# A new order for VectorE's weight work in the first slice, and half of some lower parts on GpSimd

## Chip, cores and metric

One core of one Trainium2 chip. The metric is the device time of one execution in microseconds (us), taken as the median of several runs. The engines are TensorE (PE: matmuls; PEld: its weight loads), VectorE (DVE), ScalarE (ACT), GpSimd (POOL) and SyncE (SP, which here only issues DMAs).

## What is computed

A block-wise linear attention with a decay for each head, whose result goes through a feed-forward layer with a squared ReLU. All is float32.

```python
for b in range(nb):                       # 12 blocks of 64 tokens, B=4, H=8, D=64
    intra = (qb @ kb.T * Dmask) @ vb
    inter = (qb * lam_pow) @ kv_state
    out[block] = intra + inter
    kv_state = lam_block * kv_state + (kb * rev_pow).T @ vb
x = out as (3072 tokens, 512)
h = x @ w_in                              # 512 x 2048
g = max(h, 0) ** 2
return g @ w_out                          # 2048 x 512
```

## The kernel before

TensorE multiplies in a reduced float32 format, so each operand is held as an upper part and a lower part (`wh`, `wl` for the weights, `xh`, `xl` for the activations, `gh`, `gl` for the squared ReLU), and each product is three matmuls. The tokens go through in slices of 512 (4 chunks of 128). The first slice is special: while it runs, the weights are converted too, and stay in SBUF from then on.

The first slice is a loop over 16 units, f = 0 to 15. In unit f TensorE makes the hidden block f (`hidden`, L533: 12 matmuls: four with `wh` and `xh`, four with `wh` and `xl`, and last four with `wl`), then the output products of the unit before (`project`, L563, L564, L568: 12 matmuls, with `gl` in every third), then pieces of the attention of the next slice. ScalarE makes `gh` and the square in three activations (`square`, L540 to L543), VectorE subtracts them to `gl` (`rest`, L548).

Beside this, unit f converts one lot of weights, u = f + 2: block u of w_in and the block of w_out that belongs with it, 128 x 1024 elements. The steps, with their lines in the profile:

- SyncE loads it (`wload`, L116) as 64-bit words, two DMAs of 512 KB; there are two buffers, so the load of lot u + 2 waits until the add of lot u has read its words.
- ScalarE: `first_hi` (L124), `first_lo` (L129).
- VectorE, in place in a tile `A` (every third lot lies in `pw` instead): `clamp` (L137), `shift` (L141), `sign` (L148, reads `raw` and `A`), `rounded` (L154, the add; reads `raw` and `A`).
- ScalarE: `upper` (L160, writes `wh`). VectorE: `lower` (L163, `wl` = `A` - `wh`), one unit behind the first four.

The units come in steps of four (step = f % 4), one chunk t of attention for each four: step 0 fades the state and scales the next keys on GpSimd (`fade_state` L519, `scale_k` L393), step 1 masks scores on VectorE (`masked_by_half`, L218, two instructions) and scales queries on GpSimd (`scale_q`, L401), step 2 finishes the chunk, whose results ScalarE copies out (`attend`, L499, L501, L377: five instructions) behind that unit's upper part, and loads the next chunk's 1 MB, step 3 adds the state on VectorE (`state`, L218) and the lower part of the attention's result (`low`, L378).

Every engine works through its instructions in the order of the program text; nothing reorders them. `turn` (L168) is a GpSimd copy of one element to `mark`: it reads a value that VectorE writes, and so makes what stands behind it on GpSimd wait until VectorE is that far.

Of the kernel before, what the change touches and what calls it, by code (L numbers as in the profile page):

```python
# [7 lines left out]
F32 = mybir.dt.float32  # L8
# [4 lines left out]
ALU = mybir.AluOpType  # L13
# [6 lines left out]
NCB = S // C  # L20
NT = B * NCB
DM = H * D
DF = 2048
KT = DM // P
NF = DF // P
# [6 lines left out]
NLOT = NF + 1  # L32
# [3 lines left out]
def body(ctx: ExitStack, tc: tile.TileContext, qT, kT, kvq, lam, w, out):  # L36
    nc = tc.nc
# [9 lines left out]
    V = nc.vector  # L47
# [47 lines left out]
    wh = const.tile([P, 2 * NF, DM], F32R, name="wh")  # L95
    wl = const.tile([P, 2 * NF, DM], F32R, name="wl")
# [4 lines left out]
    def lot(t, u):  # L101
        if u in (0, NF):
            return t[:, u : u + 1]
        return t.rearrange("p (s f) d -> p s f d", s=2)[:, :, u]
# [30 lines left out]
    def clamp(u):  # L135
        A = cv[u][2].bitcast(F32)
        V.tensor_scalar(out=A, in0=A, scalar1=2.0**-15, scalar2=float(LIM), op0=ALU.max, op1=ALU.min)  # L137

    def shift(u):
        A = cv[u][2]  # L140
        V.tensor_scalar(  # L141
            out=A, in0=A, scalar1=3, scalar2=0x3FFFFFFF,
            op0=ALU.logical_shift_left, op1=ALU.bitwise_and,
        )

    def sign(u):
        L, Hw, A = cv[u]
        V.scalar_tensor_tensor(  # L148
            out=A, in0=Hw, scalar=0xC0000000, in1=A, op0=ALU.bitwise_and, op1=ALU.bitwise_or
        )  # L150

    def rounded(u):
        L, Hw, A = cv[u]
        V.tensor_tensor(out=A, in0=A, in1=L, op=ALU.add)  # L154

    def whole(u):
        return cv[u][2].bitcast(F32).rearrange("p (a d) -> p a d", d=DM)

    def upper(u):
        nc.scalar.copy(lot(wh, u), whole(u))  # L160

    def lower(u):
        V.tensor_tensor(out=lot(wl, u), in0=whole(u), in1=lot(wh, u).bitcast(F32), op=ALU.subtract)  # L163
        cv.pop(u)

    def turn(u, half):
        x = cv[u][2].bitcast(F32)[0:1, 0:1] if half else wl[0:1, u, 0:1].bitcast(F32)
        nc.gpsimd.tensor_copy(mark[:, 0:1], x)  # L168
# [11 lines left out]
    def where(x, base, pattern, step, compare, fill):  # L180
# [17 lines left out]
        out=pz[:, C - T : C - T + NX], data0=s[:, 0:1].broadcast_to([P, NX]), data1=spike,  # L198
# [13 lines left out]
    for j in range(2):  # L212
# [5 lines left out]
        lambda o, x, y, op=op: V.tensor_tensor(out=o, in0=x, in1=y, op=op)  # L218
# [5 lines left out]
    b_, t_, u_, c_, d_, af = (sq[:, i, 0 : NS - 1] for i in range(6))  # L224
# [11 lines left out]
    for k in range(NS - 3, NS):  # L236
        n = 1 << k
        V.tensor_scalar(
            out=pz[:, Z + n : Z + 2 * n], in0=pz[:, Z : Z + n], scalar1=tr[:, k : k + 1], scalar2=None,
# [150 lines left out]
    def scale_k(t):  # L390
        x = tok[t][0].rearrange("p (a j) d -> p a j d", j=2)
        y = mask[:, 2:4].rearrange("p j a c -> p a j c")[:, :, :, D - 1 : D]
        nc.gpsimd.tensor_tensor(out=x, in0=x, in1=y.broadcast_to([P, NPR, 2, D]), op=ALU.mult)  # L393

    def scale_q(t):
        x = feat[t][:, 1].rearrange("p a (b c) -> p a b c", b=2)
        if t % NCB:
            y = qpow[:, 0].unsqueeze(2).broadcast_to([P, NPR, 2, D])
        else:
            x, y = x[:, :, 1], qpow[:, 0]  # L400
        nc.gpsimd.tensor_tensor(out=x, in0=x, in1=y, op=ALU.mult)  # L401
# [52 lines left out]
    def begin(t):  # L454
        begun_of[t] = [ps_a.tile([P, DM], F32, name="att") for _ in range(2)], set()
        old_state(t, 0)

    def begun_mark(t):
        c = (NPR - 1) * D
        nc.scalar.copy(mark[:, 2:3], begun_of[t][0][0][0:1, c : c + 1])  # L460
# [43 lines left out]
    def state(t, second, fades=True):  # L504

        if not second and t % NCB == NCB - 1:
            return
        u = part_of.pop(t)[:, NPR * D :].rearrange("p (a b) -> p a b", a=NPR)
        d = kv[:, :, D:] if second else kv[:, :, 0:D]
        if second and not t % NCB:  # L510
            V.tensor_copy(d, u)
        else:
            add(d, kvd, u)
        if fades and (not second or t % NCB < NCB - 1):
            fade_state(second)

    def fade_state(second):
        d = kv[:, :, D:] if second else kv[:, :, 0:D]
        nc.gpsimd.tensor_tensor(  # L519
            out=kvd, in0=d, in1=qpow[:, 0, :, D - 1 : D].broadcast_to([P, NPR, D]), op=ALU.mult  # L520
        )
# [3 lines left out]
    def hidden(m, f, xh, xl):  # L525
        h = ps_h.tile([P, N], F32, name="h")
        k = 0
        order = ((wh, xh), (wl, xh), (wh, xl))
        if m == 0 and f:
            order = order[0], order[2], order[1]  # L530
        for wt, x in order:
            for kt in range(KT):
                nc.tensor.matmul(  # L533
                    h, wt[:, f, kt * P : (kt + 1) * P], x[:, kt], start=k == 0, stop=k == 11
                )
                k += 1
        return h

    def square(h):
        nc.scalar.activation(h, h, AF.Relu)  # L540
        gh = wk.tile([P, N], F32R, name="gh")
        nc.scalar.activation(gh, h, AF.Square)
        nc.scalar.activation(h, h, AF.Square)  # L543
        return gh

    def rest(m, f, r, gh):
        gl = wk.tile([P, N], F32R, name="gl")
        V.tensor_tensor(out=gl, in0=r, in1=gh.bitcast(F32), op=ALU.subtract)  # L548
        g_of[m, f] = gh, gl
# [39 lines left out]
    def new_low(m):  # L589
        xs_of[m].append(wk.tile([P, KT, N], F32R, name="xl", tag="xl"))  # L590
# [436 lines left out]
    o, u, low = {}, {}, {}  # L1027
# [65 lines left out]
    for f in range(NF):  # L1093
        t, step, u_ = G + f // 4, f % 4, f + 2
        h = hidden(0, f, *xs_of[0])
        if step == 2:
            begin(t)
        if f == 2:
            gh = square(h)
            begun_mark(t)  # L1100
            upper(u_ - 1)
        if f < 3:
            if f < 2:
                lower(u_ - 1)
            clamp(u_)
            shift(u_)
            if f == 2:
                lower(u_ - 1)
            if f == 1:
                turn(u_, True)  # L1110
                masked_by_half(t)
                scale_q(t)
                scale_k(t + 1)
                state(t, True)
            sign(u_)
            if f != 1:
                rounded(u_)
        else:
            if u_ < NLOT:
                for op in (clamp, shift, sign):  # L1120
                    op(u_)
            if step < 3:
                upper(u_ - 1)
            if u_ < NLOT:
                rounded(u_)
            if f == 3:
                new_low(1)
            if step == 1:
                gh = square(h)
                turn(u_, True)  # L1130
                scale_q(t)
                rest(0, f, h, gh)
                masked_by_half(t)
            lower(u_ - 1)
            if u_ - 1 < NF and step != 1:
                turn(u_ - 1, False)
            if step == 3:
                state(t, False)
        wload(u_ + 2)
        if f == 0:  # L1140
            fade_state(False)
        if step == 0 and f:
            if t % NCB < NCB - 1:
                fade_state(True)
            scale_k(t + 1)
        if f < 2 or f > 2 and step != 1:
            gh = square(h)
            if step == 2:
                begun_mark(t)
        if f == NF - 1:  # L1150
            state(t + 1, True)
        if step != 1 or f == 1:
            rest(0, f, h, gh)
        if step == 3:
            low[t]()
            if f < NF - 1:
                state(t + 1, True, False)
        if f == 1:
            rounded(u_)
        if f == 0:  # L1160
            upper(u_)
        if u_ + 1 < NLOT:
            first_hi(u_ + 1)
            first_lo(u_ + 1)
        if step == 2 and u_ < NLOT:
            upper(u_)
        if prev is not None:
            project(*prev)
        prev = (0, f)
        if step == 2:  # L1170
            low[t] = attend(t)
            load_qk(t + 2)
            load_kv(t + 2)
        if f == 0:
            open_half(t)
        elif step == 0:
            scores_by_half(t, ps_a, "att")
        if f == NF - 1:
            scores_by_half(t + 1, ps_a, "att")
            scale_k(t + 2)  # L1180
# [14 lines left out]
    for j, tag in enumerate(("xh", "xl")):  # L1195
        x = wk.tile([P, 4, DM], F32, name="raws", tag=tag)
# [6 lines left out]
    def pair(i):  # L1203
        return i, first_t + 2 * i
# [6 lines left out]
    for f in range(NF):  # L1211
        t = first_t + f // 2
        h = hidden(1, f, *xs_of[1])
        behind(f, t, last_t)
        gh = square(h)
# [13 lines left out]
        if f == NF - 1:  # L1229
            x = far(*pair(3))  # L1230
# [4 lines left out]
        if f % 2 == 0:  # L1235
            go(t, t + 1 if t < last_t else None, False)
            if t == last_t:
                x = near(*pair(3), "a")
# [28 lines left out]
    for f in range(NF):  # L1267
        t = first_t + f // 2
        i, odd_ = f // 4, f // 2 % 2
        more = t < last_t  # L1270
# [95 lines left out]
```

## Time and profile before

| | |
|---|---|
| median of 3 runs | 588.33 us (586.6 to 589.16) |
| the profiled execution | 586.28 us, span 584.5 us |
| busy in the span | TensorE 572.0, VectorE 418.7, ScalarE 278.8, GpSimd 94.2 us |
| first slice, 40 to 120 us | TensorE 75.6, VectorE 77.5, ScalarE 63.6, GpSimd 12.0 of 80 us |
| 120 to 160 us | TensorE 40.0 of 40, VectorE 18.4 |
| TensorE's granted clock | 0.999 of full |
| weights' loads (`raw`) | 30 of 512 KB, 4.5 us from issue to landing (median) |
| attention loads | 512 KB (`kv_sb`) and twice 256 KB (`qk_sb`) a chunk |

A timeline row gives start, duration, engine, line and operation, written tile and read tiles, shape, and in brackets the idle time of the engine ahead of it with what ended it. Durations of neighbours overlap a little, since an instruction's record ends when its result is out; the distance from start to start is what the engine needs. Rows of several matmuls give their number behind an x.

### The profile page before, as it was taken

What the parts mean: (1) busy time and instruction counts of PE and PEld (TensorE: products, weight loads), DVE (VectorE), ACT (ScalarE), POOL (GpSimd) and SP (SyncE); (2) the same over time, 40 slices, a digit from 0 to 9 for tenths busy, and PEclk for the clock granted to TensorE, in tenths of its full rate; (3) what the DMA queues carried; (4) which work ended last, traced back from release to release, by engine and by line L of the source; (5) the groups of instructions that cost most, each with busy time, mean ns of one, the idle gap of its engine ahead of it and who ended that gap; (6) DMA issues with size and microseconds to landing.
All of it is one profiled execution on the core that took longest, in us unless ns stands there. A gap on an engine that the chain in (4) does not pass through costs nothing.

```text
span 584.5 us, 13119 instructions
## 1 busy us (share of the span) xinstructions
PE 572.0 (98%) x5276; PEld 481.7 (82%) x5276; DVE 418.7 (72%) x685; ACT 278.8 (48%) x529; POOL 94.2 (16%) x110
## 2 busy tenths in 40 slices
PE   9999899999999999999999999999999999999996
PEld 7976687778888887888888887888788888999996
DVE  5899999952688675786666668677645456997933
ACT  4698778744454455433333334445523244641510
POOL 4530110222322231000000013355100000000000
PEclk9999999999999999999999999999999999999999
DMA  8874566324599795566666643732297676766863
GB/s 298 339 254 164 183 243 217 108 74 145 197 304 351 241 305 194 159 191 208 198 199 197 199 162 121 266 123 74 74 315 230 194 195 184 248 214 204 286 206 105
DMA packets 69388, 119.35 MB, mean 204 GB/s; under 512 B 6352, under 2 KB 30928, under 8 KB 69328
## 3 DMA queue, kind: packets, MB, share of 16 engines
q1 hardware_dynamic: 66864, 115.37, 60.1%
q10 hardware_dynamic: 2464, 3.15, 1.5%
q8 instruction: 42, 0.69, 0.5%
q14 instruction: 18, 0.15, 0.1%
HBM read 88.08 MB, written 29.36 MB: 201 GB/s over the span
## 4 chain that ended last, share of the span: by engine, by line
PE 70%; DVE 19%; issue 4%; ACT 3%; DMA 2%; SPq 0%; DVEq 0%; POOL 0%; ACTq 0%; POOLq 0%
PE h L697 18%; PE acc L945 8%; PE att L697 7%; PE acc L563 6%; PE h L533 6%; PE acc L564 6%; PE acc L568 6%; PE att L945 4%; DVE wl L163 3%; PE att L440 2%; DVE A L148 2%; PE h L945 2%; DVE sums L218 2%; DVE gl L548 1%; DMA raw<-in_w 1%
## 5 line engine op out<-in xcount | busy, mean ns | idle before, releaser
L563 PE MATMUL acc<-wh,gh 128*128 128x512 f32 x256 | 101.1, 395 | 0.0
L568 PE MATMUL acc<-wh,gl 128*128 128x512 f32 x256 | 99.9, 390 | 0.0
L564 PE MATMUL acc<-wl,gh 128*128 128x512 f32 x256 | 99.8, 390 | 0.0
L697 PE MATMUL h<-wh,ring 128*128 128x512 f32 x320 | 85.8, 390 | 0.1
L540 ACT ACTIVATE h<-h 128x512 f32<-128x512 f32 x48 | 27.9, 582 | 107.3 <-PE h L533 49.0
L697 PEld LDWEIGHTS h<-wh,ring 128*128 128x128 f32 x320 | 59.9, 188 | 13.2 <-issue 0.5
L548 DVE TENSOR_TENSOR gl<-h,gh 128x512 fp32r<-128x512 f32 x48 | 33.0, 687 | 37.1 <-ACT h L543 37.1
L568 PEld LDWEIGHTS acc<-wh,gl 128*128 128x128 f32 x256 | 48.0, 188 | 11.0 <-DVE gl L548 0.9
L563 PEld LDWEIGHTS acc<-wh,gh 128*128 128x128 f32 x256 | 48.1, 188 | 10.4
L564 PEld LDWEIGHTS acc<-wl,gh 128*128 128x128 f32 x256 | 48.1, 188 | 9.6
L697 PE MATMUL h<-wl,ring 128*128 128x512 f32 x160 | 49.2, 389 | 0.0
L393 POOL TENSOR_TENSOR kv_sb<-kv_sb,pw 128x512 f32<-128x512 f32 x17 | 22.2, 1306 | 126.6 <-DMA kv_sb<-in_kvq 126.5
L519 POOL TENSOR_TENSOR kvd<-kv,pw 128x256 f32<-128x256 f32 x33 | 27.1, 822 | 83.6 <-DVE kv L218 75.2
L533 PE MATMUL h<-xh,wl 128*128 128x512 f32 x128 | 35.0, 395 | 4.4 <-DVE wl L163 4.4
L533 PE MATMUL h<-xh,wh 128*128 128x512 f32 x128 | 36.5, 407 | 0.5 <-DVE pw L218 0.2
L945 PE MATMUL acc<-folds,wh 128*128 128x256 f32 x192 | 35.2, 283 | 0.0
L697 PEld LDWEIGHTS h<-wl,ring 128*128 128x128 f32 x160 | 30.0, 188 | 6.3
L533 PE MATMUL h<-xl,wh 128*128 128x512 f32 x128 | 34.3, 390 | 0.0
L697 PE MATMUL att<-wh,ring 128*128 128x512 f32 x128 | 34.2, 389 | 0.0
L533 PEld LDWEIGHTS h<-xh,wl 128*128 128x128 f32 x128 | 23.6, 188 | 11.4 <-DVE wl L163 6.5
L218 DVE TENSOR_TENSOR wl<-sums,wh 128x1024 fp32r<-128x1024 f32 x24 | 30.4, 1265 | 1.8 <-ACT wh L917 1.8
L945 PEld LDWEIGHTS acc<-folds,wh 128*128 128x128 f32 x192 | 30.0, 192 | 0.0
(276 smaller groups left out, 1188.5 us busy)
## 6 DMA issues: line engine op xcount, KB each, us to landing
ring<-ws SPq DMA_DIRECT2D x112, 256.0 KB, 3.0
folds<-wt SPq DMA_DIRECT2D x64, 256.0 KB, 3.6
raw<-in_w SPq DMA_DIRECT2D x30, 512.0 KB, 4.5
kv_sb<-in_kvq SPq DMA_DIRECT2D x19, 512.0 KB, 5.7
ws<-parts SPq DMA_DIRECT2D x32, 256.0 KB, 4.5
qk_sb<-in_kT SPq DMA_DIRECT2D x20, 256.0 KB, 4.3
qk_sb<-in_qT SPq DMA_DIRECT2D x20, 256.0 KB, 4.4
out_x<-o SPq DMA_DIRECT2D x16, 256.0 KB, 5.1
```

What stands on the lines that cost most here:

```text
L163: V.tensor_tensor(out=lot(wl, u), in0=whole(u), in1=lot(wh, u).bitcast(F32), op=ALU.subtract)
L218: lambda o, x, y, op=op: V.tensor_tensor(out=o, in0=x, in1=y, op=op)
L393: nc.gpsimd.tensor_tensor(out=x, in0=x, in1=y.broadcast_to([P, NPR, 2, D]), op=ALU.mult)
L519: nc.gpsimd.tensor_tensor(out=kvd, in0=d, in1=qpow[:, 0, :, D - 1 : D].broadcast_to([P, NPR, D]), op=ALU.mult)
L533: nc.tensor.matmul(h, wt[:, f, kt * P : (kt + 1) * P], x[:, kt], start=k == 0, stop=k == 11)
L540: nc.scalar.activation(h, h, AF.Relu)
L548: V.tensor_tensor(out=gl, in0=r, in1=gh.bitcast(F32), op=ALU.subtract)
L563: nc.tensor.matmul(accs[m][i], gh[:, cs], wh[:, j], start=f == 0, stop=False)
L564: nc.tensor.matmul(accs[m][i], gh[:, cs], wl[:, j], start=False, stop=False)
L568: nc.tensor.matmul(accs[m][i], gl[:, cs], wh[:, j], start=False, stop=end)
L697: nc.tensor.matmul(bank, x[:, part_, kt], t[:, q + kt], start=start and z == 0, stop=stop and z == 5, skip_group_check=True,)
L945: nc.tensor.matmul(bank[:, r * 2 * P : (r + 1) * 2 * P], x, y, start=n == 0 and r == 0 and z == 0, stop=n == NQ - 1 and z == 2, skip_group ...
```

## The change

For units f >= 3 the work is written in a new order. VectorE: clamp and shift of the new lot, lower part of the last lot, sign of the new lot, `gl`, and the add at the end. The GpSimd work of each unit comes behind a `turn` that reads the new lot's tile after the shift. In steps 2 and 3 of units in which a new lot is made (f = 3, 6, 7, 10, 11, 14), GpSimd forms the w_out half of the lower part in two instructions of 128 x 256, and VectorE only the w_in half. Units 0 to 2 and everything behind the first slice stay. The line numbers move: lower is L169 on VectorE and L167 on GpSimd, `gl` L554, `turn` L174.

```diff
--- before.py
+++ after.py
@@ -159,8 +159,14 @@
     def upper(u):
         nc.scalar.copy(lot(wh, u), whole(u))
 
-    def lower(u):
-        V.tensor_tensor(out=lot(wl, u), in0=whole(u), in1=lot(wh, u).bitcast(F32), op=ALU.subtract)
+    def lower(u, shared=False):
+        x, y, z = lot(wl, u), whole(u), lot(wh, u).bitcast(F32)
+        if shared:
+            for c in range(0, DM, DM // 2):
+                cs = slice(c, c + DM // 2)
+                nc.gpsimd.tensor_tensor(out=x[:, 1, cs], in0=y[:, 1, cs], in1=z[:, 1, cs], op=ALU.subtract)
+            x, y, z = x[:, 0], y[:, 0], z[:, 0]
+        V.tensor_tensor(out=x, in0=y, in1=z, op=ALU.subtract)
         cv.pop(u)
 
     def turn(u, half):
@@ -1116,45 +1122,47 @@
             if f != 1:
                 rounded(u_)
         else:
-            if u_ < NLOT:
-                for op in (clamp, shift, sign):
-                    op(u_)
             if step < 3:
                 upper(u_ - 1)
-            if u_ < NLOT:
-                rounded(u_)
+            more = u_ < NLOT
+            if more:
+                clamp(u_)
+                shift(u_)
+                turn(u_, True)
+            if step == 0:
+                if t % NCB < NCB - 1:
+                    fade_state(True)
+                scale_k(t + 1)
+            elif step == 1:
+                scale_q(t)
+            lower(u_ - 1, step > 1 and more)
+            if more:
+                sign(u_)
+            if step == 3:
+                state(t, False)
             if f == 3:
                 new_low(1)
+            gh = square(h)
+            if step == 2:
+                begun_mark(t)
+            if f == NF - 1:
+                state(t + 1, True)
+            rest(0, f, h, gh)
             if step == 1:
-                gh = square(h)
-                turn(u_, True)
-                scale_q(t)
-                rest(0, f, h, gh)
                 masked_by_half(t)
-            lower(u_ - 1)
-            if u_ - 1 < NF and step != 1:
-                turn(u_ - 1, False)
+            if more:
+                rounded(u_)
             if step == 3:
-                state(t, False)
+                low[t]()
+                if f < NF - 1:
+                    state(t + 1, True, False)
         wload(u_ + 2)
         if f == 0:
             fade_state(False)
-        if step == 0 and f:
-            if t % NCB < NCB - 1:
-                fade_state(True)
-            scale_k(t + 1)
-        if f < 2 or f > 2 and step != 1:
+        if f < 3 and f != 2:
             gh = square(h)
-            if step == 2:
-                begun_mark(t)
-        if f == NF - 1:
-            state(t + 1, True)
-        if step != 1 or f == 1:
+        if f < 3:
             rest(0, f, h, gh)
-        if step == 3:
-            low[t]()
-            if f < NF - 1:
-                state(t + 1, True, False)
         if f == 1:
             rounded(u_)
         if f == 0:
```

VectorE before, the add of unit 6's lot and then unit 7 (lot in `A`; `wl<-pw` is the lower part of the lot before):

```order
L154 ISA pw<-raw,pw 128x2048
L163 TENSOR_TENSOR wl<-A,wh 128x2x512
L548 TENSOR_TENSOR gl<-h,gh 128x512
L137 TENSOR_SCALAR A<-A 128x1024
L141 TENSOR_SCALAR A<-A 128x1024
L148 SCALAR_TENSOR_TENSOR A<-raw,A 128x1024
L154 ISA A<-raw,A 128x2048
L163 TENSOR_TENSOR wl<-pw,wh 128x2x512
L548 TENSOR_TENSOR gl<-h,gh 128x512
```

VectorE now, unit 6's end and unit 7:

```order
L148 SCALAR_TENSOR_TENSOR pw<-raw,pw 128x1024
L554 TENSOR_TENSOR gl<-h,gh 128x512
L154 ISA pw<-raw,pw 128x2048
L137 TENSOR_SCALAR A<-A 128x1024
L141 TENSOR_SCALAR A<-A 128x1024
L169 TENSOR_TENSOR wl<-pw,wh 128x512
L148 SCALAR_TENSOR_TENSOR A<-raw,A 128x1024
L554 TENSOR_TENSOR gl<-h,gh 128x512
L154 ISA A<-raw,A 128x2048
```

The lower part has moved from behind the add to between shift and sign and has half its size here; the add (ISA) has moved to the end, behind `gl`.

GpSimd before, units 5 to 9 (the three marks are those of units 6, 7 and 8, each behind a lower part):

```order
L401 TENSOR_TENSOR qk_sb<-qk_sb,pw 128x512
L168 COPY mark<-wl 1x1 x3
L519 TENSOR_TENSOR kvd<-kv,pw 128x256
L393 TENSOR_TENSOR kv_sb<-kv_sb,pw 128x512
L168 COPY mark<-pw 1x1
L401 TENSOR_TENSOR qk_sb<-qk_sb,pw 128x4x64
```

GpSimd now, units 5 to 9:

```order
L407 TENSOR_TENSOR qk_sb<-qk_sb,pw 128x512
L174 COPY mark<-pw 1x1
L167 TENSOR_TENSOR wl<-A,wh 128x256 x2
L174 COPY mark<-A 1x1
L167 TENSOR_TENSOR wl<-pw,wh 128x256 x2
L174 COPY mark<-A 1x1
L525 TENSOR_TENSOR kvd<-kv,pw 128x256
L399 TENSOR_TENSOR kv_sb<-kv_sb,pw 128x512
L174 COPY mark<-pw 1x1
L407 TENSOR_TENSOR qk_sb<-qk_sb,pw 128x4x64
```

Two pieces of `wl` stand behind the marks of units 6 and 7, and every mark now reads the lot's tile, not `wl`.

ScalarE's order is the same in both. From unit 6 to unit 7, with the first conversion pair of lot 9, the upper part of lot 8 (which waits for that lot's add) and the attention's copies ahead of unit 7's activations:

```order
L124 ACTIVATE A<-raw 128x1024
L129 ACTIVATE raw<-raw 128x1024
L160 CAST wh<-pw 128x2x512
L505 COPY a<-att 128x2x64
L507 COPY a<-att 64x2x64 x2
L505 COPY a<-att 128x2x64
L507 COPY a<-att 64x2x64 x2
L383 CAST xh<-a 128x4x128
L546 ACTIVATE h<-h 128x512
```

Nothing has moved here but the moment at which VectorE has the upper part's input ready.

## Rows read from the trace of the kernel before

**Rows 1.** Windows: length, busy us of PE, PEld, DVE, ACT, POOL, clock, DMA share, GB/s.

```profile
40.00:120.00 80.00, 75.60 (x639) 58.90 (x638) 77.47 (x92) 63.55 (x99) 12.01 (x22) 1.00 0.51 178
```

**Rows 2.** TensorE's waits, 40 to 75 us, then 75 to 120: sum, times, longest.

```profile
PE h L533 <- DVE wl L163: 3.2, 3, 2.1
...
PE h L533 <- DVE wl L163: 1.2, 2, 0.9
```

**Rows 3.** Timeline of TensorE: `wl` matmuls of units 6, 7; `gl` reads; unit 14.

```profile
65.94 1.20 PE L533 MATMUL h<-xh,wl 128*128 128x512 f32 x4 [2.10 <-DVE wl L163]
...
73.68 1.07 PE L533 MATMUL h<-xh,wl 128*128 128x512 f32 x4
...
80.48 0.39 PE L568 MATMUL acc<-wh,gl 128*128 128x512 f32 x1
...
105.78 0.39 PE L568 MATMUL acc<-wh,gl 128*128 128x512 f32 x1
...
114.34 1.07 PE L533 MATMUL h<-xh,wh 128*128 128x512 f32 x4
```

**Rows 4.** Timeline of VectorE: unit 2 in part, unit 4, masks of unit 5.

```profile
41.12 0.69 DVE L141 TENSOR_SCALAR A<-A 128x1024 uint32<-128x1024 uint32 x1
41.73 1.22 DVE L163 TENSOR_TENSOR wl<-A,wh 128x1024 fp32r<-128x1024 f32 x1
42.86 1.22 DVE L148 SCALAR_TENSOR_TENSOR A<-raw,A 128x1024 uint32<-128x1024 uint32 x1
...
52.86 0.68 DVE L137 TENSOR_SCALAR A<-A 128x1024 f32<-128x1024 f32 x1
53.58 0.69 DVE L141 TENSOR_SCALAR A<-A 128x1024 uint32<-128x1024 uint32 x1
54.31 1.23 DVE L148 SCALAR_TENSOR_TENSOR A<-raw,A 128x1024 uint32<-128x1024 uint32 x1
55.67 1.23 DVE L154 CUSTOM_DVE_ANT_0 A<-raw,A 128x2048 uint16<-128x2048 uint16 x1
56.81 1.22 DVE L163 TENSOR_TENSOR wl<-pw,wh 128x1024 fp32r<-128x1024 f32 x1
57.95 0.69 DVE L548 TENSOR_TENSOR gl<-h,gh 128x512 fp32r<-128x512 f32 x1
58.55 1.35 DVE L137 TENSOR_SCALAR A<-A 128x1024 f32<-128x1024 f32 x1
...
63.77 0.75 DVE L218 TENSOR_TENSOR a<-att,pw 128x256 f32<-128x256 f32 x2
```

**Rows 5.** Timeline, VectorE and GpSimd side by side in unit 1; GpSimd alone, unit 5.

```profile
36.38 1.66 DVE L148 SCALAR_TENSOR_TENSOR A<-raw,A 128x1024 uint32<-128x1024 uint32 x1
...
35.68 1.28 POOL L401 TENSOR_TENSOR qk_sb<-qk_sb,pw 128x512 f32<-128x512 f32 x1
36.93 2.04 POOL L393 TENSOR_TENSOR kv_sb<-kv_sb,pw 128x512 f32<-128x512 f32 x1
...
58.16 0.17 POOL L168 COPY mark<-wl 1x1 f32<-1x1 f32 x1 [6.10 <-DVE wl L163]
58.30 1.05 POOL L393 TENSOR_TENSOR kv_sb<-kv_sb,pw 128x512 f32<-128x512 f32 x1
```

**Rows 6.** Timeline of ScalarE: upper part to last activation of unit 3; conversions.

```profile
45.37 1.05 ACT L160 CAST wh<-A 128x1024 fp32r<-128x1024 f32 x1 [1.63 <-DVE A L154]
...
49.63 0.60 ACT L543 ACTIVATE h<-h 128x512 f32<-128x512 f32 x1
...
61.86 1.18 ACT L124 ACTIVATE pw<-raw 128x1024 f32<-128x1024 f32 x1 [0.84 <-DMA raw<-in_w]
...
63.95 1.04 ACT L160 CAST wh<-A 128x1024 fp32r<-128x1024 f32 x1
```

**Rows 7.** Instructions of tile `raw`, 30 to 125 us: the loads' time to landing.

```profile
DMA to landing us min/median/max: 3.3/4.5/6.1
```

## The prediction

> **What bounds the kernel now.** I read the stages first. Between 40 and 120 us VectorE is busy for 77.5 of 80 us and TensorE for 75.6 [rows 1]; this is the first slice from its 2nd hidden unit to its 14th, in which every unit makes one lot of weights. Behind 122 us TensorE hardly waits for anybody, so whatever it gains before that it keeps to the end. Then the waits of TensorE: all of them in that stretch are for `wl`, the lower parts that VectorE writes, 3.2 us in three before 75 us and 1.2 us in two behind it [rows 2]. The longest is in unit 6, and after each the four matmuls need 1.20 us where undisturbed ones need 1.07 [rows 3]. The most that any order of VectorE can give back here is therefore 4.4 + 5 x 0.13 = 5.0 us.
>
> Why `wl` is late: VectorE does clamp, shift, sign, add on the new lot and only then the lower part of the last one [rows 4]. In units 5, 9 and 13 even `gl` and the two masks stand in front of it.
>
> **What the new order does, term by term.** I call R(f) the moment at which the add of unit f ends. One row pair gives what two dependent instructions cost: clamp to shift 0.72, shift to sign 0.73, sign to add 1.36, while shift to an independent lower part takes 0.61 and lower part to sign 1.13 [rows 4]. An add to the next, independent, instruction takes 1.14, and I take 1.14 for sign to `gl`, which is independent too. So a plain unit goes from 5.69 us (52.86 to 58.55 [rows 4]) to 0.72 + 0.61 + 1.13 + 1.14 + 0.60 + 1.15 = 5.35 us: 0.34 us saved, because no step follows its own input directly. The lower part ends 2.5 us into the unit, not 5.1, and `gl` starts at 3.6. That alone removes the three waits before 75 us: 3.2 + 3 x 0.13 = 3.6 us gained for TensorE.
>
> **GpSimd's halves.** Half a lower part is half of 1.13, so 0.55 us off VectorE in six units. But VectorE and GpSimd hold each other up. GpSimd's `qk_sb` runs from 35.68 for 1.28 us, VectorE's sign, started at 36.38, takes 1.66 instead of 1.23, and GpSimd's next multiply takes 2.04 where it needs 1.05 alone: each stands until the other's whole instruction is over, and the one that waits gets the next turn [rows 4, 5]. So a half on GpSimd costs VectorE what it saves, unless it falls beside `gl` (0.60 us), whose input in PSUM was not held up by anything. Who goes first behind the lower part decides. If the one-element mark copy (0.17 us [rows 5]) also has to wait for the lower part's end, sign comes directly behind it and the real GpSimd work falls beside `gl`: 0.17 us lost a unit, 0.6 where the 1.05 multiply overhangs `gl` by 0.45. If it doesn't, GpSimd's first operation stands in line during the lower part and goes ahead of sign: 0.5 to 1.28 us a unit. No row shows a mark copy beside an instruction of this kind. I take the first, since all the other GpSimd operations do wait, and keep the second as a bound. The Trainium skill, SBUF — State Buffer, section "SBUF: two separate sides", says that the port pair is an exclusive lock, held for a whole instruction, also between a VectorE operation with two SBUF inputs and a GpSimd operation that reads SBUF. The trace agrees (1.66 for 1.23), and by that rule the mark copy, which reads one element, waits too; where it holds, the sum is the first one, otherwise the second.
>
> **What is late next.** The add moves to the unit's end, and two things hang on it. The load of the lot after next takes the buffer that the add releases: it is asked for at R. From the add's end at 55.67 + 1.23 = 56.90 to the ScalarE instruction that waited for that load it is 4.96 us (61.86), and the two conversions take 2.09 (to 63.95) [rows 4, 6]. Then ScalarE's upper part (1.05, the first row of [rows 6]) must come before the lower part. So lower(f+2) starts no earlier than R(f) + 4.96 + 2.09 + 1.05 = R(f) + 8.1. Before, the add ended 4.0 us into the unit, not 5.4 (52.86 to 56.90 [rows 4]), and this chain had slack. In units 7 and 11 ScalarE has more in line: behind the upper part stand the five attention copies and the three activations, 4.86 us from 45.37 to 50.23 with nothing between [rows 6]. There `gl` starts at R(f) + 4.96 + 2.09 + 4.86 = R(f) + 11.9, and the add ends 0.60 + 1.23 later.
>
> Now the sum, with the first bound and in brackets the second. I leave unit 4 starting where it does, 52.9. It lasts 5.35 + 0.6 (1.05); unit 5 reaches its add's end after 0.72 + 0.61 + 1.13 + 1.14 + 0.60 + 0.66 for the masks [rows 4] + 1.23 = 6.1, plus 0.17 (1.28): R(5) = 65.1 (66.7). `gl` of unit 7 starts at 77.0 (78.6) and ends 0.69 later, 77.7 (79.3). TensorE reads it at 80.48 now [rows 3] and would like it 3.6 us sooner, 76.9: it waits, and 2.8 (1.2) us of its gain are left. Four units on: R(7) = 78.8 (80.4). R(9) = R(7) + 8.1 + 1.13 + 1.14 + 0.60 + 0.66 + 1.23 + 0.17 (0.7) = 91.8 (94.0). `gl` of unit 11 ends 12.6 later, 104.4 (106.6), against 105.78 now: 1.4 (-0.8) left. So these four units take 26.7 us in the new order; TensorE without waits needs 105.78 - 80.48 less the one wait between, about 24.9. R(11) = 105.5 (107.7). The upper part of lot 14 is there 8.1 later, 113.6 (115.8); TensorE begins that unit at 114.34 now: 0.7 (-1.5) left. Last comes the wait in unit 14, 0.9 of the 1.2 us [rows 2], with its restart 1.05: the lower part is then ready before it is read, so this is gained in full. Total 1.8 (-0.5). Where GpSimd's multiply blocks the clamp of unit 9, some 0.6 us more is lost. I take **1.5 us gained**.
>
> The profiled execution is 586.28 us (span 584.5), 2.05 below the median 588.33. The sum makes 584.8 of it, and 586.8 of the median.
>
> **Rivals.** (a) *TensorE loses none of it.* If the loads land faster than the one I could time, ScalarE has upper part 8 ready earlier and the chain never binds. The quickest landing is 3.3 us against a median of 4.5 [rows 7]; 1.2 us less in each of the four steps from R(5) to lot 14 is 4.8, more than is lacking. Then all 5.0 us come: 583.3. For it: all waits now are for `wl`, and that moves by 2.5 us. Against it: 4.96 us was measured on a load with no other traffic near.
>
> (b) *GpSimd goes ahead of sign in every unit*: the brackets, 0.5 us slower, 588.8.
>
> (c) *Slower: the loads land late.* The longest landing is 6.1 us [rows 7]. The weights are now asked for nearer to the 1 MB of attention loads that SyncE issues in the same unit. With 1.6 us more in each of four steps the gain of 1.5 becomes a loss of 4.9: 593.2. It decides from some 1.1 us a step on, a landing of 5.6. Against it: only one load in four is near the attention's.
>
> **How the numbers follow.** Forecast 0.45, (a) 0.22, (b) 0.24, (c) 0.09. This kernel's measurement tells some 0.5% (2.9 us) from no change. Faster by more needs 585.4: (a) and the near edge of the forecast, 0.30. Slower by more needs 591.3: (c), 0.09. The rest, 0.61. For 8 in 10 the range takes in (a) and (b) with the runs' own spread of 1.3 us either way, and leaves (c) out: 583.2 to 590.0.
>
> **What the changed profile would show.** Step by step: TensorE's waits for `wl` between 40 and 75 us gone; a plain unit on VectorE near 5.4 us; instead VectorE's `gl` in units 7 and 11 waits for ScalarE's activation by about 1.5 us or more; the ScalarE conversions wait for the weights' DMA, which they hardly did; TensorE waits for `gl` and for the upper part there, about 3 us in sum; SyncE's issue of the weights stands at the end of a unit. Wrong would be: VectorE without idle time in units 7 and 11 (then (a)), sign of 1.8 us and more behind every lower part (then (b)), conversions that start over 6 us after the add (then (c)), or TensorE waiting after 125 us where it does not now.

## The result: slower

The changed kernel takes 592.84 us (median of 5 runs, 591.88 to 593.6) against 587.26 for the kernel before: 1.0084 times as long, 95% interval 1.0061 to 1.0106. I had forecast 586.8, which was 1.5 us under the 588.33 known then, and a range up to 590.0. The profiled execution takes 592.87 us with a span of 591.1, 6.6 longer than the 584.5 of before.

Most of it is in the first slice: unit 15's first matmul starts at 128.87 us, before at 123.06, which is 5.8 of the 6.6 us. Behind it the execution is 0.8 us longer than before (462.2 against 461.4); I have not followed that. The waits of TensorE from 20 to 170 us (instruction and tile, who was waited for: sum, times, longest), to be held against [rows 2]:

```profile
PE att L446 <- DVE a L224: 4.5, 3, 1.7
PE att L446 <- ACT mark L466: 2.7, 3, 1.8
PE acc L574 <- DVE gl L554: 2.5, 3, 1.3
PE h L539 <- DVE pw L224: 0.2, 1, 0.2
```

The waits for `wl`, 4.4 us before, are all gone, as the new order meant. In their place stand 9.7 us for other things in that slice. The largest is one that my prediction doesn't name: `a L224`, the masks of units 5, 9 and 13. `ACT mark` is a copy of one element out of the bank in which an attention has begun, which ScalarE makes behind the activations of units 6, 10 and 14; the attention's next matmuls write that bank and wait for it. The waits for `gl` are for that of units 4, 8 and 12.

VectorE and GpSimd in unit 4, as [rows 4] and [rows 5] show them for before (start, duration, instruction; rows of the two engines apart):

```profile
53.28 0.69 DVE L137 TENSOR_SCALAR A<-A 128x1024 f32<-128x1024 f32 x1
54.00 0.69 DVE L141 TENSOR_SCALAR A<-A 128x1024 uint32<-128x1024 uint32 x1
54.61 1.22 DVE L169 TENSOR_TENSOR wl<-pw,wh 128x1024 fp32r<-128x1024 f32 x1
55.90 2.07 DVE L148 SCALAR_TENSOR_TENSOR A<-raw,A 128x1024 uint32<-128x1024 uint32 x1
57.89 0.68 DVE L554 TENSOR_TENSOR gl<-h,gh 128x512 fp32r<-128x512 f32 x1
58.49 1.21 DVE L154 CUSTOM_DVE_ANT_0 A<-raw,A 128x2048 uint16<-128x2048 uint16 x1
59.63 0.68 DVE L137 TENSOR_SCALAR A<-A 128x1024 f32<-128x1024 f32 x1
...
54.83 1.04 POOL L174 COPY mark<-A 1x1 f32<-1x1 f32 x1 [3.60 <-DVE A L141]
55.83 1.05 POOL L399 TENSOR_TENSOR kv_sb<-kv_sb,pw 128x512 f32<-128x512 f32 x1
```

The mark copy, 0.17 us elsewhere, takes 1.04: it stands until the lower part (54.61 to 55.83) is over. Then GpSimd's multiply starts at once, and sign, 1.23 us by itself, takes 2.07: it stands until that multiply is over at 56.88. Sign overwrites the tile that the mark reads, so it also waits for the mark: it starts 1.29 us behind the lower part's start (in [rows 4] 1.13), and 0.07 behind the multiply's. So the unit lasts 6.35 us, not 5.35 and not 5.69. In unit 6, with GpSimd's two halves:

```profile
68.17 0.69 DVE L169 TENSOR_TENSOR wl<-A,wh 128x512 fp32r<-128x512 f32 x1
68.93 2.42 DVE L148 SCALAR_TENSOR_TENSOR pw<-raw,pw 128x1024 uint32<-128x1024 uint32 x1
...
68.39 0.50 POOL L174 COPY mark<-pw 1x1 f32<-1x1 f32 x1 [4.95 <-DVE pw L141]
68.86 1.41 POOL L167 TENSOR_TENSOR wl<-A,wh 128x256 fp32r<-128x256 f32 x2
```

Both halves run in front of sign: VectorE saves 0.53 us on the lower part and loses 1.2 on sign. Over the units 3 to 13 sign takes 1.74 to 2.65 us, where before it took 1.22 or 1.23; the excess is 10.3 us in sum.

What the moved add does is seen in the chain of work that ended last, within 58 to 79 us (start, length, what):

```profile
58.57 1.14 DVE A L154
...
59.78 0.33 SPq L116
...
60.16 4.64 DMA raw<-in_w
...
64.88 1.14 ACT pw L124
66.01 1.07 ACT raw L129
67.08 0.24 SPq L116
...
67.37 4.81 DMA raw<-in_w
...
72.25 1.14 ACT A L124
73.39 1.06 ACT raw L129
74.44 0.93 ACT wh L160
```

It is the chain of the prediction: add, issue of the load, landing, two conversions, upper part, and then the attention's copies and activations up to the `gl` of unit 7 at 79.18. At 67.08 the view follows the second of the load's two DMAs and puts it to the conversion that ended just then; the first is issued at 67.00, behind the add of unit 5, which ended at 66.93. ScalarE waits for the weights' DMA 13.5 us in seven places; before, it was 1.3 in three, of which [rows 6] shows the longest.

### The profile page after: what moved, and what is told of

It is laid out like the page before. It is cut to its first block, busy times and chain, and to the rows that moved or that the text cites. A ratio compares the mean times of both kernels' runs of the same rounds, so it can differ in the third digit from the quotient of the medians.

```text
span 591.1 us, 13124 instructions
## 1 busy us (share of the span) xinstructions
PE 572.5 (97%) x5276; PEld 482.4 (82%) x5276; DVE 423.2 (72%) x685; ACT 278.5 (47%) x529; POOL 112.2 (19%) x122
## 4 chain that ended last, share of the span: by engine, by line
PE 71%; DVE 12%; ACT 6%; DMA 5%; issue 4%; POOL 1%; SPq 0%; DVEq 0%; ACTq 0%; POOLq 0%
PE h L703 18%; PE acc L951 7%; PE att L703 7%; PE h L539 6%; PE acc L569 6%; PE acc L574 6%; PE acc L570 6%; PE att L951 4%; DMA raw<-in_w 3%; PE att L446 2%; DMA ws<-parts 2%; PE h L951 2%; DVE sums L224 1%; DVE A L154 1%; DVE gl L554 1%
## 5 line engine op out<-in xcount | busy, mean ns | idle before, releaser
L554 DVE TENSOR_TENSOR gl<-h,gh 128x512 fp32r<-128x512 f32 x48 | 32.9, 686 | 39.0 <-ACT h L549 39.0
L569 PEld LDWEIGHTS acc<-wh,gh 128*128 128x128 f32 x256 | 48.1, 188 | 10.3
L399 POOL TENSOR_TENSOR kv_sb<-kv_sb,pw 128x512 f32<-128x512 f32 x17 | 20.8, 1221 | 127.8 <-DMA kv_sb<-in_kvq 127.7
L224 DVE TENSOR_TENSOR wl<-sums,wh 128x1024 fp32r<-128x1024 f32 x24 | 30.4, 1265 | 1.8 <-ACT wh L923 1.8
L548 ACT ACTIVATE gh<-h 128x512 fp32r<-128x512 f32 x48 | 28.8, 599 | 1.5
```

The source lines that it names most:

```text
L569: nc.tensor.matmul(accs[m][i], gh[:, cs], wh[:, j], start=f == 0, stop=False)
```

## Experiments

Three theories. **P**, the port: GpSimd's work behind shift holds up sign. **L**, the loads: the add at the unit's end makes loads and conversions late. **M**, the masks: TensorE waits for them since the next attention begins in the banks of PSUM (the memory that TensorE writes) that they read. The kernel before ran beside each, at 586.6 to 587.1 us median; ratios are against it.

| run | what is changed | median us | ratio, 95% |
|---|---|---|---|
| the change | | 592.84 | 1.0061 to 1.0106 |
| e1_no_half | change without GpSimd's halves | 591.31 | 1.0055 to 1.0105 |
| e17_mark_apart | change, sign doesn't wait for the mark | 591.52 | 1.0055 to 1.0108 |
| e4_masks_early | change, masks behind shift | 591.04 | 1.0048 to 1.0092 |
| e11_no_loads | change, loads of lots 9 to 16 left out | 590.30 | 1.0047 to 1.0083 |
| e3_pool_late | change, GpSimd's work behind sign | 588.14 | 1.0007 to 1.0031 |
| e5_pool_late_no_half | e3 without halves | 587.32 | 0.9991 to 1.0030 |
| e16_late_no_loads | e3, loads of lots 9 to 16 left out | 584.76 | 0.9959 to 0.9984 |
| e9_beside_gl | no halves; masks and scale_q behind shift, other GpSimd work behind sign | 589.11 | 1.0026 to 1.0055 |
| e10_add_first | e9, add ahead of gl | 587.52 | 1.0006 to 1.0032 |
| e19_q_by_masks | e3, masks and scale_q behind the lower part | 589.45 | 1.0027 to 1.0069 |
| e18_mixed | e19 without halves, add ahead of gl in half of the units | 588.24 | 1.0013 to 1.0042 |
| e2_half_only | before, with GpSimd's halves | 588.86 | 1.0019 to 1.0049 |
| e15_before_step1 | before; in units 5, 9, 13 masks and scale_q behind shift, lower part ahead of gl | 587.16 | 0.9993 to 1.0019 |

### One part alone, and one part away

**e1_no_half**: the call without its second argument.

```diff
-            lower(u_ - 1, step > 1 and more)
+            lower(u_ - 1)
```

> The changed kernel with VectorE writing the whole lower part in every unit, GpSimd's halves left out; the order and the marks as changed. Theory P (the port: what GpSimd has in line behind the mark goes ahead of sign and holds it up): sign in units 3, 6 and 14 falls from 2.4 to about 1.7 us, in 7, 10, 11 from 1.75 to 1.6, the lower part rises from 0.69 to 1.22; in sum VectorE neither gains nor loses, 591.5 to 593.5, and steps 0 and 1 keep their sign of 2.1 to 2.6. Theory L (the add at the unit's end makes the loads late and that is all of the loss): no change either, 592 to 593. If the halves themselves are the loss: back to 587.

4.3 us slower than before, against 5.6: within its error the halves neither make nor mend the loss. Sign in unit 6 fell to 1.22 (no GpSimd work is left behind that mark), the lower part rose to 1.22; in steps 0 and 1 sign stayed at 1.74 to 2.65. The direction is theory P's, though sign fell further than the 1.7 that I expected, and the time is just under my range. The time alone does not divide P from L, which expected no change either.

**e2_half_only**: the old order, with `lower(u_ - 1, step > 1 and u_ < NLOT)`.

> The kernel before with GpSimd's halves alone, VectorE in its old order (and GpSimd's marks as before). The halves are ready to run from the upper part on, beside clamp, shift, sign and add. Theory P: each of the two holds up VectorE by some 0.55 us, 1.1 lost for 0.55 saved in six units: 1 to 4 us slower than before, 588 to 591. Theory L: the add stays where it was, so no slower than before, 584 to 588.

1.9 us slower. TensorE's waits for `wl` rise from 4.4 to 5.4. In the old order the halves run beside shift and sign of the next lot; the pair starts at 93.34:

```profile
93.81 1.11 DVE L141 TENSOR_SCALAR A<-A 128x1024 uint32<-128x1024 uint32 x1
94.95 1.64 DVE L148 SCALAR_TENSOR_TENSOR A<-raw,A 128x1024 uint32<-128x1024 uint32 x1
...
93.34 2.16 POOL L167 TENSOR_TENSOR wl<-pw,wh 128x256 fp32r<-128x256 f32 x2 [1.57 <-ACT wh L160]
```

Shift loses 0.42 and sign 0.41, against 0.54 saved on the lower part, as theory P expected.

### GpSimd's work behind sign

**e3_pool_late**: mark, fades, scalings and halves (`lower_rest`) move down by two VectorE instructions.

```diff
                 clamp(u_)
                 shift(u_)
+            lower(u_ - 1, step > 1 and more)
+            if more:
+                sign(u_)
                 turn(u_, True)
             if step == 0:
...
             elif step == 1:
                 scale_q(t)
-            lower(u_ - 1, step > 1 and more)
-            if more:
-                sign(u_)
+            if step > 1 and more:
+                lower_rest(u_ - 1)
```

> The changed kernel with the mark, all GpSimd work of the unit and the halves behind sign instead of behind shift, so that they start beside gl; VectorE's order as changed. Theory P: sign falls to 1.23 us everywhere, the add or the next clamp is held up instead by what is left over; a unit is 0.5 to 1 us shorter, gl and masks come sooner: 586 to 589. Theory L: the add still ends the unit and the loads are as late: 590 to 593.

1.2 us slower than before, so 4.4 of the 5.6 us are back by this move alone. Unit 4 again:

```profile
56.27 1.22 DVE L148 SCALAR_TENSOR_TENSOR A<-raw,A 128x1024 uint32<-128x1024 uint32 x1
57.41 0.68 DVE L559 TENSOR_TENSOR gl<-h,gh 128x512 fp32r<-128x512 f32 x1
58.01 1.89 DVE L154 CUSTOM_DVE_ANT_0 A<-raw,A 128x2048 uint16<-128x2048 uint16 x1
...
57.76 1.05 POOL L404 TENSOR_TENSOR kv_sb<-kv_sb,pw 128x512 f32<-128x512 f32 x1
```

Sign is 1.22 in all units. The multiply hides beside `gl` as far as `gl` lasts, and the add takes the rest (1.89 instead of 1.22). The masks are early enough now. What TensorE still waits for:

```profile
PE att L451 <- POOL qk_sb L412: 3.0, 3, 1.2
PE att L451 <- ACT mark L471: 2.9, 4, 1.3
PE h L544 <- ACT wh L160: 0.7, 2, 0.4
PE acc L579 <- DVE gl L559: 0.4, 1, 0.4
```

`qk_sb` are the queries, whose scaling the move has made late; the next two come through ScalarE. P holds for most of the loss, though not all of the 4.4 us is its own: with shorter units the adds, and so the loads, come sooner too (unit 5's add ends at 66.11, in the changed kernel at 66.93).

**e5_pool_late_no_half**: the same without halves.

> The kernel of e3_pool_late (mark and GpSimd's work behind sign) with VectorE writing the whole lower part in every unit, no halves. It asks what the halves are worth where GpSimd's work doesn't stand in front of sign. If they save VectorE 0.55 us in six units and fall beside gl: e5 is 1 to 2.5 us slower than e3_pool_late, 589 to 590.5. If what they save comes back as an add held up (1.5 us and more instead of 1.22): the same as e3_pool_late, 587.5 to 588.7.

587.32 against 588.14, with intervals that overlap: where GpSimd doesn't stand in front of sign, no gain from the halves shows. A part of the 0.53 us that one saves comes back in the add (1.50 to 1.56 us in units 3, 6 and 10 with them, 1.22 without).

**e17_mark_apart**: the mark of the changed kernel reads a copy, so that sign, which overwrites what the mark reads, has no wait for it.

```diff
+    def note(u):
+        V.tensor_copy(mark[:, 3:4], cv[u][2].bitcast(F32)[0:1, 0:1])
+        nc.gpsimd.tensor_copy(mark[:, 0:1], mark[:, 3:4])
...
-                turn(u_, True)
+                note(u_)
```

> The changed kernel, but the mark no longer reads the lot's tile, which sign writes: VectorE copies one element of it to a place of its own behind shift, and the mark reads that. GpSimd's work stands where it did, only sign waits for nobody any more. Theory W (sign waits for the mark, since it overwrites what the mark reads; the mark waits for the lower part's end, and the work behind the mark starts before the signal is back at VectorE): sign now gets in behind the mark, 1.3 to 1.4 us in most units instead of 1.75 to 2.65; of the 4.5 us that moving GpSimd's work behind sign gave back at least half comes back here, at a price of about 0.2 us a unit for the copy: 588 to 590.5. Theory P alone (whoever waited longer gets the port, marks or not): sign stays at 1.75 to 2.65 and the copies come on top: 593 to 595.

4.7 us slower, between the two forecasts: theory W, the wait, is not the whole cause. Without it sign gets in first in units 3, 4 and 12 (1.21 us) and in no other (1.76 to 2.80). VectorE's signs of units 4 and 5, and GpSimd's marks there:

```profile
56.07 1.21 DVE L148 SCALAR_TENSOR_TENSOR A<-raw,A 128x1024 uint32<-128x1024 uint32 x1
...
62.06 2.44 DVE L148 SCALAR_TENSOR_TENSOR A<-raw,A 128x1024 uint32<-128x1024 uint32 x1
...
55.14 2.18 POOL L178 COPY mark<-mark 1x1 f32<-1x1 f32 x1 [3.78 <-DVE mark L177]
...
61.06 1.11 POOL L178 COPY mark<-mark 1x1 f32<-1x1 f32 x1 [2.73 <-DVE mark L177]
```

At 56.07 sign starts on time and the mark stands until it is over as well (2.18); at 62.06 it is the other way round. Both wait for the same lower part. In the three units in which sign came first the mark starts 0.20 us after the lower part has begun, in the six in which all GpSimd work did, 0.13 or 0.14. Why this should decide stays open. In the changed kernel that distance is 0.22, so there the wait for the mark may have its share; no run shows how much.

### The loads

**e11_no_loads**: the lots from 9 on take the words of lots 7 and 8 instead of a load; **e16_late_no_loads** does the same to e3.

```diff
+            if u > 8:
+                raw[u] = kept_raw[7 + (u - 9) % 2][:, 0 : len(x) * DM]
+                return
...
+            kept_raw[u] = raw[u]
```

> The changed kernel with the loads of the lots 9 to 16 left out: the words of lots 7 and 8 are converted again, so w_in and w_out are wrong from there on; nothing else changes. ScalarE's conversions then wait for no DMA. Theory L: what came from late loads goes, that is TensorE's waits for ScalarE's mark (2.7 us) and what VectorE idled (about 6 us from unit 7 to 13): 587 to 589.5. Theory P: VectorE is as long behind shift as before and stays the bound: 591 to 593.

> The kernel of e3_pool_late (GpSimd's work behind sign) with the loads of lots 9 to 16 left out, so that lots 7 and 8 are converted again and the weights are wrong from there on. Theory P and L together (the two are the whole loss): what e3_pool_late still waits for ScalarE's mark (2.9 us) and the upper part (0.7) shrinks to 1 us or less, scale_q's 3.0 us stay: 584.5 to 586.5. Theory P alone (the loads cost nothing by themselves): as e3_pool_late, 587.5 to 588.5.

Without loads the change is still 3.7 us slower than before (a gain of 1.9 on the change): too slow for L alone, faster than P alone allows. e16 is 584.76, 3.4 us faster than e3 and 2.1 faster than before. So leaving the loads out is worth some 2 us while GpSimd keeps sign back (the intervals of this run and the change overlap) and 3.4 once it doesn't. TensorE's waits in e16:

```profile
PE att L455 <- ACT mark L475: 2.1, 3, 1.4
PE att L455 <- POOL qk_sb L416: 1.4, 2, 1.0
PE h L548 <- ACT wh L164: 0.3, 1, 0.3
```

Its unit 15 starts at 122.07 on TensorE, 1.0 us before the old kernel's 123.06. The span is 1.8 shorter; where the other 0.8 comes from behind unit 15 I have not followed. These two runs also take the loads' traffic away, not only their lateness, and the kernel before was not run without loads, so they bound what L costs and do not measure it.

### Masks, queries and the add's place

**e4_masks_early** moves `masked_by_half(t)` from behind `gl` to between shift and lower part.

> The changed kernel with the two masks of units 5, 9 and 13 between shift and lower part instead of behind gl. TensorE waited 4.5 us for these masks in the changed kernel. Theory M (the masks free the PSUM banks in which the next unit's attention begins, so where they stand decides): these waits are gone, and since scale_q runs beside the masks sign falls to 1.3 us there: 587 to 589.5. Theory L: the waits move to the next thing that VectorE is late with: 591 to 593.

4.1 us slower, 1.5 better than the change. The masks' waits are gone, as theory M says:

```profile
PE att L446 <- ACT mark L466: 5.0, 3, 2.7
PE acc L574 <- DVE gl L554: 1.9, 2, 1.1
PE h L539 <- DVE wl L169: 1.4, 2, 0.7
```

But the total, 8.3, is nearly the old 9.7: the next late things take their place. Sign is 1.21 in units 5, 9 and 13 now, but `scale_q` outlasts the masks, and the lower part behind them takes 2.07, 1.50 and 2.06. So M is where the loss shows, not what makes it.

**e9_beside_gl** (mark, masks and `scale_q` behind shift in units 5, 9, 13; the rest of GpSimd's work behind sign; no halves), **e10_add_first** (its add ahead of `gl`), **e19_q_by_masks** (e3 with masks and `scale_q` behind the lower part) and **e18_mixed** try to keep the order and lose nothing.

```text
 e9:                                       e19:
     shift(u_)                                 shift(u_)
     turn(u_, True)   # step 1                 lower(u_ - 1, ...)
     masked_by_half(t)                         turn(u_ - 1, False)   # step 1
     scale_q(t)                                masked_by_half(t)
     lower(u_ - 1)                             scale_q(t)
     sign(u_)                                  sign(u_)
 e10: rounded(u_) ahead of rest(0, f, h, gh)
 e18: as e19 without halves, rounded(u_) ahead of rest(...) in steps 0 and 1
```

> VectorE's order as changed, no halves; in units 5, 9, 13 the mark, the two masks and scale_q directly behind shift, so that scale_q runs beside the masks; in all other units the mark and the GpSimd work behind sign, beside gl. In the run with all GpSimd work behind sign TensorE waited 3.0 us for scale_q and 2.9 for ScalarE's mark. Theory P (the port is the loss): nothing is held up any more, all of the order's gain comes: 583 to 585. Theory L (the add at the unit's end makes the weights' loads late, ScalarE waits for them, and gl, upper part and the mark of TensorE's attention come late): the scale_q waits go, those for ScalarE stay or grow: 585.5 to 587.5, the conversions wait 1.5 to 2.5 us for their loads.

> As the kernel of e9_beside_gl, but with the add directly behind sign and gl (in which GpSimd's work is to run) behind the add. The add then ends 0.5 to 0.6 us earlier in a unit, gl 1.3 later, and GpSimd's work is beside the add, which it holds up. Theory L: loads are asked for sooner and the conversions wait less, but gl is late: the same or up to 2 us faster than e9_beside_gl. Theory P: the add waits for GpSimd, up to 1 us a unit: 1 to 4 us slower than e9_beside_gl.

> The kernel of e3_pool_late with units 5, 9 and 13 changed: behind the lower part the mark (it reads the finished wl), the two masks and scale_q beside them, then sign, gl, add. TensorE's 3.0 us of waits for scale_q should go, the loads stay late. By the waits: 2 to 3 us faster than e3_pool_late, 585 to 586.2, which is faster than before by up to 0.3 per cent. If ScalarE's mark and gl are late by then anyway: 587 to 588.

> No halves. All units: clamp, shift, whole lower part. Units 5, 9, 13: then the mark (which reads the finished wl, so nobody waits for it), the masks with scale_q beside them, sign, add, gl. Units 4, 8, 12: sign, add, then mark and GpSimd's work beside gl. Other units: sign, mark, gl, add. By P and L: loads are asked for 0.6 to 1.2 us sooner in half of the units, masks and scale_q are early, nothing is held up: better than e9_beside_gl (589.1) and e10_add_first (587.5), and if the sum is right faster than before: 584 to 586. If gl behind the add is what TensorE then waits for, as in e10_add_first (4.0 us): 587 to 588.

None beats the kernel before. In e9 sign is 1.21 or 1.22 in units 3 to 13, yet it is 2.5 us slower: TensorE waits 4.2 us for ScalarE's mark and ScalarE 13.9 for the weights.

```profile
PE att L446 <- ACT mark L466: 4.2, 3, 1.7
...
61.02 2.07 DVE L169 TENSOR_TENSOR wl<-A,wh 128x1024 fp32r<-128x1024 f32 x1
...
60.72 1.30 POOL L407 TENSOR_TENSOR qk_sb<-qk_sb,pw 128x512 f32<-128x512 f32 x1
```

So P, as far as it speaks of sign, is not the only cause. GpSimd is still in VectorE's way, though, in other places: lower parts, adds and clamps take 4.7 us too long in sum, the lower part of unit 5 above among them. In the kernel before, lower parts, clamps and shifts lose 3.1, so of e9's loss P in a wider sense is not excluded. e10 differs in the add's place alone and is 1.6 us faster than e9 although `gl` is later (4.0 us of waits for it); that is L's sign, though the two intervals overlap a little. e19 lost what I expected it to gain: the waits for `scale_q` went, those for ScalarE's mark rose from 2.9 to 4.9 us, since its add in units 5, 9, 13 comes even later. e18, with half of the adds early, waits 5.2 us for `gl` instead. What one place gives another takes.

**e15_before_step1** leaves the old order but for units 5, 9 and 13.

> The kernel before with units 5, 9 and 13 alone changed: mark, masks and scale_q directly behind shift, then sign, add, lower part, gl (before: sign, add, gl, masks, lower part). The lower part ends 0.6 us (gl) and 0.24 us (scale_q that held it up) sooner there, and gl 1.8 us later. Of TensorE's 4.4 us of waits 3.3 stand behind these units. If each shrinks by 0.84: 1.5 to 2.5 us faster than before, 584.5 to 585.5. If gl is then late instead: the same as before, 586.5 to 587.5.

No difference that can be told (interval 0.9993 to 1.0019): `scale_q` behind the masks now delays sign there (2.08 us in unit 5), so the lower part comes hardly sooner (its end is at 65.52 in unit 5, before at 65.89, and at 117.43 in unit 13, before at 117.18); the waits for `wl` are 4.9 us in sum.

## Why the prediction was wrong, point by point

- **That `wl` stops being waited for**: right. All 4.4 us went.
- **That those 3.6 us are gained for TensorE before unit 7**: wrong, and the first step that failed. I followed TensorE's reads of `wl`, `gl` and `wh` and left out `begin`, the attention that starts in units 6, 10 and 14 in the banks of the masks. The masks stand behind lower part, sign and `gl` now, and the first of the two ended at 65.47 in unit 5; the lower part that TensorE waited for before ended at 65.89. So the wait of 2.10 us in [rows 3] became one of 1.67 for the masks, in the same place:

```profile
65.06 0.74 DVE L224 TENSOR_TENSOR a<-att,pw 128x256 f32<-128x256 f32 x2
...
65.61 0.69 PE L446 MATMUL att<-qk_sb,kv 64*64 64x64 f32 x16 [1.67 <-DVE a L224]
```

- **GpSimd and VectorE hold each other up for whole instructions**: right. The mark stands behind the lower part, 1.04 us for 0.17, as the Trainium skill says of the port pair (SBUF — State Buffer, "SBUF: two separate sides": an exclusive lock, held for the whole instruction). The trace agrees.
- **That sign then comes directly behind the mark**: wrong, and the largest term. I made the mark's wait the test for who is next; the mark did wait, and GpSimd's work was next all the same, 0.84 us in unit 4, 1.2 in unit 6, 1.4 in unit 8 (sign 2.64). What I left out is that GpSimd's next instruction starts as soon as the mark ends, 0.07 us before sign, which waits for the mark, can; e17 shows that this is not all of it. The bracketed bound had GpSimd ahead of sign, at up to 1.28 a unit, as a case of its own with 0.24, and its sign of being wrong, a sign of 1.8 us and more, came in most units. Moving GpSimd's work behind sign (e3) gave 4.4 us back.
- **The chain add, load, conversions, upper part**: right in kind, under-sized. In the changed kernel the conversion starts 5.2 us after the add in unit 4 (59.70 to 64.88), 5.3 in unit 5 (66.93 to 72.25) and 5.75 in unit 8 (88.85 to 94.60), against my 4.96 from one row [rows 6]. `gl` of unit 7 came at 79.18, the bracket had 78.6. ScalarE's waits for loads, which I expected, are there (13.5 us), and with them the `gl` of unit 7 waits for ScalarE's activation, by 1.40.
- **The bracket's total of 0.5 us slower**: wrong by 5 us although most of its dates came within 2 us (R(5) 66.9 for 66.7, `gl` of unit 11 108.5 for 106.6). The sum follows TensorE to three things: `gl` of unit 7, `gl` of unit 11 and the upper part of lot 14. TensorE hardly waited for any of them. It read the first at 79.92, still 0.56 us sooner than before (the bracket had 1.2), and that of unit 11 at 109.56, 3.8 later than before (the bracket had 0.8). The loss came in between and behind, in waits that the sum has no term for: the masks of units 9 and 13 (1.10 and 1.71), `gl` of unit 8 behind a sign of 2.64, and ScalarE's mark in unit 10, ahead of which a conversion had waited 3.05 us for its load:

```profile
79.92 0.50 PE L574 MATMUL acc<-wh,gl 128*128 128x512 f32 x1
...
87.77 0.50 PE L574 MATMUL acc<-wh,gl 128*128 128x512 f32 x1 [1.26 <-DVE gl L554]
...
99.46 0.39 PE L446 MATMUL att<-qk_sb,kv 64*64 64x64 f32 x6 [1.82 <-ACT mark L466]
```

- **Rival (c), loads landing late**: not the cause; the landings took 4.6 us in the median and 6.1 at most (before, 4.5 and 6.1), and without the loads from lot 9 on the change is still 3.7 us slower. The loads were late because they were asked for later, not because they took longer.
- **The order's own gain**: a part of it may be what shows once both obstacles are gone (e16, 2.1 us of the 5.0), with 3.8 us of waits left, of which 1.4 for the queries that e3 itself made late. But e16 lacks loads that the kernel before has, so the gain is not shown for the order alone.

## To carry to other kernels

In these runs work on GpSimd was free only beside VectorE instructions that take an operand from PSUM (in e3's unit 4 `gl` takes 0.68 us and the multiply 1.05, as alone); clamp, shift, sign, add and lower part each stood for whole GpSimd instructions. So place such work beside the first kind, count it as serial anywhere else, and do not count on which of the two goes first. When an order is changed so that one operand comes sooner, list every operand that the waiting engine reads until it is back at the same place, buffers that become free among them; the next one sets the time, and here it came only 0.4 us sooner than the first had. Before moving an instruction that frees a load's buffer, follow the chain of load, conversion and copy on other engines that hangs on it: without those loads the new order was 1.9 and 3.4 us faster (e11, e16), and with the add ahead of `gl` again 1.6 (e10).

## What the runs showed of the hardware

A copy of one element on GpSimd, 0.17 us alone, took 1.04 behind a VectorE instruction with two SBUF inputs, and 2.18 where a second such instruction came directly behind the first (e17). Which engine gets the turn when both wait for the end of the same instruction was not the same each time: sign came first in units 3, 4 and 12 of e17 and GpSimd's work in units 5, 6, 8, 9, 10 and 13, with the same kinds of instruction in front; the mark had started 0.20 us after the lower part began in the former and 0.13 or 0.14 in the latter. Two GpSimd instructions back to back let a waiting VectorE instruction in between in units 7, 10 and 11 of the changed kernel (sign 1.74 to 1.76, the pair 2.90 to 2.92 us) and not in units 3, 6, 8 and 12 (sign 2.42 to 2.65).
